# First weights and a head's inputs over a second DMA queue, with three more conversion ticks and one more head ahead of the first slot

## The chip, the cores and the metric

The kernel runs on one core of a Trainium2 chip. The core has TensorE (PE in the profile, with PEld for its weight loads), VectorE (DVE), ScalarE (ACT), GpSimd (POOL) and SyncE (SP), which here only issues DMAs. The metric is the device time of one execution in microseconds. Of the kernel before, three runs gave 1000.1 (median), 998.52 and 1000.47.

## The reference, cut to what matters

Three stages follow each other. Causal attention over 4 batches, 8 heads, 576 positions and head size 64, with an extra bias made of running sums:

```python
scores = scale * np.matmul(q, k.transpose(0, 1, 3, 2))
cum = np.cumsum(np.maximum(s, 0.0), axis=-1)
bias = -(cum[:, :, :, None] - cum[:, :, None, :])
scores = np.where(causal, -1e9, scores + np.minimum(bias, 0.0))
attn = softmax(scores)          # row maximum taken off, 1e-9 added to the sum
x = np.matmul(attn, v)          # heads side by side: 2304 tokens x 512
```

Then two feed-forward layers, 512 to 2048 to 512 each, over the 2304 tokens: the first with `g = h * clip(h + 3, 0, 6) / 6`, the second with `g = h * sigmoid(h)`. The weights come in as 64-bit floats.

## The kernel before, in words

**Weights.** A layer's two matrices are cut into 16 chunks of rows each, called i0 to i15 and o0 to o15. A chunk of the first layer is 128 x 512 64-bit words, 512 KB. It is loaded raw by one DMA (line 147), and then turned into a high and a low 32-bit part: ScalarE takes the two 32-bit halves apart (lines 159 and 160), GpSimd makes the sign (line 161), VectorE joins them (lines 172 and 176), ScalarE rounds the high part (line 120) and VectorE forms the low part (line 187). The class `Feed` does this as a pipeline: one call of `tick` (line 200) loads a new chunk, takes apart the chunk of three ticks ago, joins the one of four ticks ago and splits the one of five ticks ago. So the first three ticks only issue loads. The intermediate `mag` tiles come from a pool of three.

**Attention.** The 4 x 8 heads are each cut in two parts, A (positions 0 to 255) and B (the rest), and are worked through one per slot. A head's inputs are loaded by `load` (q, k and v, three DMAs for the first 14 heads, lines 413, 414 and 403) and `load_cum` (the running sums, line 423, from the on-chip tile `pairs` for heads 0 to 3, from its copy `pair_d` in memory after that). In `slot` (line 787) a head goes through its scores (line 512), the masked row minimum (line 534), the exponential (line 552), transposes (line 580) and the product with v (line 687). The tile `pairs` is written by VectorE (line 349) and ScalarE (line 350) from a scan of s (line 345).

**Order.** Nine slots hold attention only. Their number of ticks comes from a rate of 0.4 a slot; afterwards each slot has two ticks, and beside its head a step of the first layer: `first` (lines 260 to 262) multiplies by an i chunk, `gate_high` and `gate_low` make the activation, `second` (lines 299 to 301) multiplies by an o chunk. When the heads have run out, the rest of the first layer and then the whole second layer follow, all on TensorE. Before all that, line 91 issues 34 matmuls on a constant tile, and slots without a step issue three more each (line 825). `split_rows` (line 352) writes six rows of running sums to memory (line 365), for use by later heads.

**Queues.** Every DMA ahead of the very end is issued by SP, in one order, and all transfers use one queue. The head inputs of the first 14 heads lie in the places of chunks 8 to 15, and the tiles of the running sums in places of chunks 6, 7 and 15, so the raw loads of those chunks come after their use. The order of instructions on each engine is made by a list scheduler: an instruction that is ready in the scheduler's model can be placed ahead of one that stands earlier in the source (the cast of line 362, which stands behind slot 9, runs at 4.96 us).

Of the kernel before, what the change touches and what calls it, by code (L numbers as in the profile page):

```python
# [11 lines left out]
I32 = mybir.dt.int32  # L12
# [15 lines left out]
def kernel(  # L28
# [15 lines left out]
    nc = tc.nc  # L44
# [85 lines left out]
    class Chunk:  # L130
        def __init__(self, kind, m, f):
            self.key = (kind, m, f)
            self.src = ((w1i, w1o), (w2i, w2o))[m][kind == "o"][f]
            self.nm = f"{kind}{m}_{f}"
            self.home = wpool, f"{kind}{f}"
# [2 lines left out]
            pool, tag = self.home  # L138
            return pool.tile(shape, dt, tag=tag, name=f"{name}{self.nm}")

        def load(self):
            if self.src.dtype == F32:
                self.val = self.place([P, DM], F32, "raw")
                nc.sync.dma_start(self.val, self.src)
            else:
                raw = self.place([P, 2 * DM], I32, "raw")
                nc.sync.dma_start(raw, self.src.bitcast(I32))
                words = raw.rearrange("p (n two) -> p n two", two=2)
                self.words = words[:, :, 0], words[:, :, 1]

# [38 lines left out]
    class Feed:  # L189


        def __init__(self, keys, hi_eng, lo_eng):
            self.ch = [Chunk(*k) for k in keys]
            self.hi_eng, self.lo_eng = hi_eng, lo_eng
            self.t = 0

        def done(self):
            return self.t >= len(self.ch) + 3 + 2

        def tick(self):  # L200
            n = len(self.ch)
            t = self.t - 3
            lo = self.lo_eng[t % len(self.lo_eng)] if 0 <= t - 2 < n else ""
            if lo:
                self.ch[t - 2].high(self.hi_eng[t % len(self.hi_eng)])
            if 0 <= t < n:
                self.ch[t].fields()
            if lo == "p":
                self.ch[t - 2].low(lo)
            if 0 <= t - 1 < n:  # L210
                self.ch[t - 1].join()
            if lo == "v":
                self.ch[t - 2].low(lo)
            if self.t < n:
                self.ch[self.t].load()
            self.t += 1


# [133 lines left out]
    def split_rows():  # L352

        def row(tag, name):
            return wpool.tile([BH, S], F32R, tag=tag, name=name)

        f = NF - 1
        hi, lo = row(f"i{f}", "cumh"), row(f"o{f}", "cuml")
        one, neg = row(f"i{NF // 2 - 2}", "one"), row(f"i{NF // 2 - 1}", "neg")
        nc.gpsimd.memset(f32(one), 1.0)  # L360
        nc.gpsimd.memset(f32(neg), -1.0)
        nc.scalar.copy(hi, crow)
        nc.vector.tensor_tensor(out=lo, in0=crow, in1=f32(hi), op=ALU.subtract)
        for r, t in enumerate((one, one, hi, lo, neg, neg)):
            nc.sync.dma_start(f32(rows_d[:, r, :]), f32(t))
# [4 lines left out]
    class Head:  # L370
# [20 lines left out]
                    (c, 0, w // 2, False), (c, w // 2, w, True)]  # L391
            self.full = [c for c in self.chunks if c < NFULL]

        def load(self):
            b, h, nm, nk, nq = self.b, self.h, self.nm, self.nk, self.nq
            if self.at < 14:

                t = wpool.tile([P, 2 * DM], F32, tag=spare[self.at], name=f"in{nm}")
                self.q2, self.k2 = t[:, :nq], t[:, nq : nq + nk]
                self.qk = t[:, : nq + nk]  # L400
                self.va = t[:, DM + nk :][:, : self.nkc * D].rearrange("p (c d) -> p c d", d=D)
                self.load_qk()
                nc.sync.dma_start(self.va, v1[b, h, :, : self.nkc, :])
                return
            tags = ("qs", "kl") if self.whole and self.slot else ("q2", "k2")
            self.q2 = apool.tile([P, nq], F32, tag=tags[0], name=f"q2{nm}")
            self.k2 = apool.tile([P, nk], F32, tag=tags[1], name=f"k2{nm}")
            self.load_qk()

        def load_qk(self):  # L410
            b, h, nk = self.b, self.h, self.nk
            for r in (slice(0, D), slice(D, 2 * D))[: 1 if self.whole else 2]:
                nc.sync.dma_start(self.q2[r, :], qT[b, h, :, self.q0 : nk])
                nc.sync.dma_start(self.k2[r, :], kT[b, h, :, :nk])

        def load_cum(self):

# [356 lines left out]
    heads = []  # L774
# [3 lines left out]
    feed = Feed([(kd, 0, f) for f in range(NF) for kd in "io"], "a", "v")  # L778
# [3 lines left out]
    def ticks(n):  # L782
        for _ in range(n):
            if not feed.done():
                feed.tick()
# [79 lines left out]
    def at(i):  # L865
        return heads[i] if 0 <= i < len(heads) else None


    loaded = 2
    for hd in heads[:loaded]:  # L870
        hd.load()
    ticks(3)
    for hd in heads[:loaded]:
        hd.load_cum()
    nc.sync.dma_start(pair_d, pairs)
    heads[0].places()
    k = 0
    p1 = p2 = None
    plan = [(True, False)] * (H + 1) + [(i < 55, True) for i in range(68)]
    nslot = 0  # L880
    for has_head, has_step in plan:
        cur = at(k) if has_head else None
        nx = at(k + 1) if has_head else None
        loads = []
        while has_head and loaded < len(heads) and loaded <= k + (
            2
        ):
            loads.append(heads[loaded])
            loaded += 1
        k += has_head and cur is not None  # L890
        tk = [0, 0, 0, 0]
        if not feed.done():
            rate = ((0.4,)*9+(2,))[min(nslot, len(((0.4,)*9+(2,))) - 1)]
            for i in range(4):
                feed_at += rate / 4
                tk[i] = int(feed_at)
                feed_at -= tk[i]
        slot(cur, p1, p2, nx, loads, has_step, tk)
        if nslot == 9:
            split_rows()  # L900
        p1, p2 = cur, p1
        nslot += 1
        if nslot == H + 1:
            p2.av_sum()
            p2 = None
            split1(0)
            turns["s"] = turns["s"][:1]
        if has_step and step in first_step[1:NB1]:
            blk = first_step.index(step)
            assert k - (cur is not None) >= (blk + 1) * H  # L910
            if p2:
                p2.av_sum()
                p2 = None
            if blk == NB1 - 1:
                cx.close()
                xpool = cx.enter_context(
                    tc.tile_pool(name="xlast", bufs=1, side="right", reuse_waits="tile")
                )
            split1(blk)
            if blk == NB1 - 1:  # L920
                break
# [70 lines left out]
    feed = Feed([("o", 1, f) for f in range(NF)], "a", "v")  # L992
# [293 lines left out]
```

## Time and profile before

| | |
|---|---|
| median of three runs | 1000.1 us |
| profiled execution | 1000.54 us, its span 998.8 us |
| PE busy | 970.8 us (97%) |
| DVE busy | 737.9 us (74%) |
| ACT busy | 511.0 us (51%) |
| POOL busy | 317.2 us (32%) |
| DMA moved | 125.41 MB, mean 126 GB/s |

The span runs from the first to the last instruction; the profiled execution's own time has 1.7 us around it. The busy shares are means over stages of very different kind, so the table alone does not say which engine a stage waits for. A busy PE can be one that multiplies a constant tile.

### The profile page before, as it was taken

Reading aid. Unit: us, or ns where it says so; the run is one execution under the profiler, and the core shown is the slowest. Engines: PE = TensorE matmul, PEld = TensorE weight load, DVE = VectorE, ACT = ScalarE, POOL = GpSimd, SP = SyncE. Lnnn points to the kernel's source line nnn. Section 1 sums busy time; section 2 is a strip of 40 time slices with the busy share of each in tenths; the row PEclk is TensorE's granted clock in tenths of the full one; section 3 lists DMA queues with packets and bytes.
Section 4 is the critical chain, followed back from the end, with each engine's and each line's share of the span. In section 5 each row is a group of like instructions: output and inputs, shape, how many; then the busy total and the mean of one; then the engine's idle time right before and its main releaser. Section 6 shows DMA issues by size and latency. Waiting matters only on the chain.

```text
span 998.8 us, 17929 instructions
## 1 busy us (share of the span) xinstructions
PE 970.8 (97%) x6268; PEld 891.6 (89%) x6268; DVE 737.9 (74%) x1757; ACT 511.0 (51%) x1177; POOL 317.2 (32%) x323
## 2 busy tenths in 40 slices
PE   8899989999999999999999999999999999999997
PEld 5789979999999999999997877899988989889996
DVE  6899998888789888988866799887574434743343
ACT  6898554555455555555446656564443323432332
POOL 4457853443333443434425566532000000000000
PEclk9999999999999999999999999999999999999999
DMA  5796112312222223222215957434354233442421
GB/s 174 225 302 198 47 40 67 92 46 63 83 77 75 71 59 92 60 64 80 60 39 186 392 212 237 163 116 190 133 195 169 77 145 110 167 154 76 148 74 64
DMA packets 54419, 125.41 MB, mean 126 GB/s; under 512 B 12332, under 2 KB 34076, under 8 KB 51000
## 3 DMA queue, kind: packets, MB, share of 16 engines
q1 hardware_dynamic: 53880, 123.60, 37.3%
q8 instruction: 50, 0.82, 0.3%
q10 hardware_dynamic: 448, 0.66, 0.2%
q14 instruction: 41, 0.34, 0.1%
HBM read 99.52 MB, written 24.69 MB: 124 GB/s over the span
## 4 chain that ended last, share of the span: by engine, by line
PE 70%; DVE 11%; DMA 8%; issue 4%; POOL 4%; SPq 3%; ACT 1%; POOLq 0%; DVEq 0%; ACTq 0%
PE a L1083 6%; PE a L1084 6%; PE a L1085 6%; PE h L1066 5%; PE h L1068 5%; PE h L1067 5%; PE ph L260 4%; PE ph L261 4%; PE ph L262 4%; PE acc L299 4%; PE acc L300 4%; PE acc L301 4%; PE poB L672 4%; DMA rawi<-in_w1i_dram 3%; POOL rawo L161 2%
## 5 line engine op out<-in xcount | busy, mean ns | idle before, releaser
L260 PE MATMUL ph<-xh,wi 128*128 128x256 f32 (+1 forms) x512 | 154.1, 303 | 3.2 <-DVE g L273 3.1
L300 PE MATMUL acc<-gl,wo 128*128 128x256 f32 (+1 forms) x512 | 151.1, 297 | 2.4 <-DVE gl L280 2.4
L261 PE MATMUL ph<-xl,wi 128*128 128x256 f32 (+1 forms) x512 | 151.6, 296 | 0.0
L262 PE MATMUL ph<-xh,wi 128*128 128x256 f32 (+1 forms) x512 | 151.3, 296 | 0.0
L301 PE MATMUL acc<-gh,wo 128*128 128x256 f32 (+1 forms) x512 | 149.8, 294 | 0.0
L1125 ACT ACTIVATE gh<-h 128x384 fp32r<-128x384 f32 x96 | 50.3, 524 | 185.4 <-DVE h L1133 185.3
L299 PE MATMUL acc<-gh,wo 128*128 128x256 f32 (+1 forms) x512 | 143.8, 297 | 0.0
L1083 PE MATMUL a<-wo,gh 128*128 128x512 f32 x288 | 113.5, 394 | 1.4 <-ACT gh L1125 0.9
L1084 PE MATMUL a<-wo,gh 128*128 128x512 f32 x288 | 113.1, 393 | 0.0
L260 PEld LDWEIGHTS ph<-xh,wi 128*128 128x128 f32 x512 | 97.4, 190 | 8.9 <-DVE g L273 2.5
L300 PEld LDWEIGHTS acc<-gl,wo 128*128 128x128 f32 x512 | 96.4, 188 | 6.4 <-DVE gl L280 3.5
L262 PEld LDWEIGHTS ph<-xh,wi 128*128 128x128 f32 x512 | 97.6, 191 | 3.0
L261 PEld LDWEIGHTS ph<-xl,wi 128*128 128x128 f32 x512 | 97.5, 190 | 3.2
L301 PEld LDWEIGHTS acc<-gh,wo 128*128 128x128 f32 x512 | 96.5, 189 | 3.3
L299 PEld LDWEIGHTS acc<-gh,wo 128*128 128x128 f32 x512 | 95.6, 189 | 3.4
L161 POOL TENSOR_SCALAR rawi<-rawi 128x512 int32<-128x512 f32 x32 | 70.0, 2188 | 74.1 <-ACT magi L160 48.4
L1085 PE MATMUL a<-wo,gl 128*128 128x512 f32 x288 | 90.0, 392 | 0.0
L161 POOL TENSOR_SCALAR rawo<-rawo 128x512 int32<-128x512 f32 x32 | 74.5, 2329 | 48.0 <-ACT mago L160 46.3
L1127 DVE TENSOR_TENSOR gl<-h,gh 128x384 fp32r<-128x384 f32 x96 | 53.8, 560 | 39.9 <-ACT h L1126 38.2
L114 POOL TENSOR_SCALAR gh<-g 128x512 fp32r<-128x512 f32 x68 | 50.6, 745 | 92.6 <-DVE g L273 77.4
L1133 DVE TENSOR_TENSOR h<-h,u 128x384 f32<-128x384 f32 x72 | 40.1, 557 | 53.5 <-PE h L1068 53.2
L1066 PE MATMUL h<-x0t,w 128*128 128x384 f32 x192 | 64.9, 338 | 0.7 <-DVE u L1133 0.7
(220 smaller groups left out, 2554.6 us busy)
## 6 DMA issues: line engine op xcount, KB each, us to landing
w<-w_d SPq DMA_DIRECT2D x18, 1792.0 KB
w_d<-w SPq DMA_DIRECT2D x8, 1792.0 KB
k2B<-in_kT_dram SPq DMA_DIRECT2D x64, 144.0 KB
rawi<-in_w1i_dram SPq DMA_DIRECT2D x16, 512.0 KB
rawo<-in_w1o_dram SPq DMA_DIRECT2D x16, 512.0 KB
rawi<-in_w2i_dram SPq DMA_DIRECT2D x16, 512.0 KB
rawo<-in_w2o_dram SPq DMA_DIRECT2D x16, 512.0 KB
q2B<-in_qT_dram SPq DMA_DIRECT2D x64, 80.0 KB
```

The lines of the kernel that those rows point to most:

```text
L161: nc.gpsimd.tensor_scalar(out=high, in0=f32(high), scalar1=0.0, scalar2=float(SIGN), op0=ALU.is_lt, op1=ALU.mult,)
L260: nc.tensor.matmul(o, wih[:, cs], xh[c], start=c == 0, stop=False)
L261: nc.tensor.matmul(o, wih[:, cs], xl[c], start=False, stop=False)
L262: nc.tensor.matmul(o, wil[:, cs], xh[c], start=False, stop=c == NDC - 1)
L299: nc.tensor.matmul(a, woh[:, cs], gh[:, jj, :], start=b0, stop=False)
L300: nc.tensor.matmul(a, woh[:, cs], gl[:, jj, :], start=False, stop=False)
L301: nc.tensor.matmul(a, wol[:, cs], gh[:, jj, :], start=False, stop=b1)
L1066: nc.tensor.matmul(ps, w[:, 0, cs], xh[:, c, :], start=c == 0, stop=False)
L1083: nc.tensor.matmul(accs[t], gh[:, k, cs], woh, start=b0, stop=False)
L1084: nc.tensor.matmul(accs[t], gh[:, k, cs], wol, start=False, stop=False)
L1085: nc.tensor.matmul(accs[t], gl[:, k, cs], woh, start=False, stop=b1)
L1127: nc.vector.tensor_tensor(out=gl[:, i, o], in0=g, in1=f32(gh[:, i, o]), op=ALU.subtract)
```

## The change

The loads get a queue as an argument. Before the first slot, head 0 and head 2 load over SP's queue and head 1 over ScalarE's. All raw chunks that are loaded before the tenth slot go over ScalarE's queue; afterwards over SP's again. Three ticks precede the loads of the running sums as before, and three more follow them, ahead of slot 0, so that six ticks are done instead of three and six raw chunks are loaded instead of three. Until 14 heads are loaded, a slot loads the head three ahead instead of two. `split_rows` comes behind the eighth slot instead of the tenth.

```diff
-        def load(self):
+        def load(self, queue=nc.sync):
             if self.src.dtype == F32:
                 self.val = self.place([P, DM], F32, "raw")
-                nc.sync.dma_start(self.val, self.src)
+                queue.dma_start(self.val, self.src)
             else:
                 raw = self.place([P, 2 * DM], I32, "raw")
-                nc.sync.dma_start(raw, self.src.bitcast(I32))
+                queue.dma_start(raw, self.src.bitcast(I32))
...
+            self.queue = nc.sync
...
-                self.ch[self.t].load()
+                self.ch[self.t].load(self.queue)
...
-                self.load_qk()
-                nc.sync.dma_start(self.va, v1[b, h, :, : self.nkc, :])
+                self.load_qk(queue)
+                queue.dma_start(self.va, v1[b, h, :, : self.nkc, :])
...
-                nc.sync.dma_start(self.q2[r, :], qT[b, h, :, self.q0 : nk])
-                nc.sync.dma_start(self.k2[r, :], kT[b, h, :, :nk])
+                queue.dma_start(self.q2[r, :], qT[b, h, :, self.q0 : nk])
+                queue.dma_start(self.k2[r, :], kT[b, h, :, :nk])
...
-    loaded = 2
-    for hd in heads[:loaded]:
-        hd.load()
+    loaded = 3
+    feed.queue = nc.scalar
+    for hd, queue in zip(heads, (nc.sync, nc.scalar, nc.sync)):
+        hd.load(queue)
     ticks(3)
     for hd in heads[:loaded]:
         hd.load_cum()
     nc.sync.dma_start(pair_d, pairs)
+    ticks(3)
     heads[0].places()
...
-        while has_head and loaded < len(heads) and loaded <= k + (
-            2
-        ):
+        while has_head and loaded < len(heads) and loaded <= k + 2 + (loaded < 14):
...
-        if nslot == 9:
+        if nslot == 7:
             split_rows()
...
         if nslot == H + 1:
+            feed.queue = nc.sync
             p2.av_sum()
```

## Rows read from the trace of the kernel before

**Rows 1.** The page: share of the chain that ended last, by engine

```profile
PE 70%; DVE 11%; DMA 8%; issue 4%; POOL 4%; SPq 3%; ACT 1%; POOLq 0%; DVEq 0%; ACTq 0%
```

**Rows 2.** Windows of seven stretches: start and end, length, busy time by engine

```profile
core 0: us, PE busy (x) PEld busy (x) DVE busy (x) ACT busy (x) POOL busy (x), PEclk, DMA share, GB/s
0.00:5.00 5.00, 3.56 (x9) 1.34 (x10) 2.78 (x5) 1.63 (x3) 3.67 (x17) 1.00 0.25 68
5.00:12.03 7.03, 6.68 (x31) 3.06 (x29) 1.14 (x3) 3.48 (x7) 1.95 (x2) 1.00 0.86 290
12.03:31.10 19.07, 15.93 (x110) 12.51 (x108) 16.77 (x71) 15.71 (x50) 8.49 (x5) 1.00 0.51 140
31.10:40.00 8.90, 7.76 (x58) 6.63 (x57) 7.78 (x29) 7.85 (x23) 3.47 (x2) 1.00 0.84 249
40.00:80.00 40.00, 36.87 (x280) 34.65 (x279) 38.57 (x119) 37.42 (x94) 24.93 (x13) 0.96 0.91 284
80.00:150.50 70.50, 63.24 (x496) 59.29 (x494) 69.12 (x156) 45.46 (x105) 47.04 (x34) 0.98 0.29 87
150.50:998.80 848.30, 836.75 (x5295) 774.13 (x5295) 601.75 (x1381) 399.44 (x900) 227.62 (x254) 1.00 0.35 119
```

**Rows 3.** Chain of waits around 150 us: start, length, what

```profile
149.88 0.61 DVE g L273
150.48 0.04 issue
150.53 0.38 PE ph L260
```

**Rows 4.** Timeline of PE, two places: start, length, engine, line, work, idle before

```profile
1.45 9.63 PE L86 MATMUL idle<-busy 128*128 128x512 bf16 x34 [1.45 <-DVE half L101]
11.42 0.46 PE L512 MATMUL ps0A<-inA 66*128 66x128 f32 x2 [0.35 <-DMA rawi<-in_w1i_dram]
...
27.34 0.46 PE L512 MATMUL ps0A<-inA 66*128 66x128 f32 x2 [1.45 <-DMA inA<-pair_d]
```

**Rows 5.** Timeline of SP, the DMA issues, from the start

```profile
0.73 0.41 SPq L341 DMA_DIRECT2D irow<-in_s_dram  x1
1.20 0.58 SPq L413 DMA_DIRECT2D inA<-in_qT_dram  x1
1.83 0.58 SPq L414 DMA_DIRECT2D inA<-in_kT_dram  x1
2.45 0.58 SPq L403 DMA_DIRECT2D inA<-in_v_dram  x1
...
4.86 0.43 SPq L147 DMA_DIRECT2D rawi<-in_w1i_dram  x1
...
6.42 1.39 SPq L423 DMA_DIRECT2D inA<-pairs  x2
...
35.41 0.78 SPq L365 DMA_DIRECT2D rows_d<-one  x2
...
37.25 0.84 SPq L365 DMA_DIRECT2D rows_d<-neg  x2
```

**Rows 6.** Timeline of ACT and POOL before the first slot

```profile
0.72 1.28 ACT L350 ACT_TABLE_LOAD   x1 [0.72 <-PEq L1267]
4.65 0.40 ACT L350 COPY pairs<-orow 32x256 f32<-32x256 f32 x1 [2.65 <-DVE orow L345]
9.02 0.67 ACT L159 ACTIVATE rawi<-rawi 128x512 int32<-128x512 uint32 x1 [3.39 <-DMA rawi<-in_w1i_dram]
10.33 2.00 POOL L161 TENSOR_SCALAR rawi<-rawi 128x512 int32<-128x512 f32 x1 [5.08 <-DMA rawo<-in_w1o_dram]
```

**Rows 7.** Timeline of DVE, opening and head 7

```profile
2.64 0.60 DVE L342 TENSOR_SCALAR irow<-irow 32x576 f32<-32x576 f32 x1 [1.25 <-DMA irow<-in_s_dram]
12.03 0.29 DVE L534 CUSTOM_DVE_ANT_0 pb0A<-ps0A,cmask 128x128 f32<-128x128 f32 x1 [5.62 <-PE ps0A L512]
12.37 1.13 DVE L172 SCALAR_TENSOR_TENSOR magi<-magi,rawi 128x512 int32<-128x512 int32 x1
...
25.36 0.69 DVE L187 TENSOR_TENSOR wo<-mago,wo 128x512 fp32r<-128x512 f32 x1
25.96 0.28 DVE L694 TENSOR_TENSOR xtA<-poA,sums 128x128 f32<-128x128 f32 x1
27.84 0.29 DVE L534 CUSTOM_DVE_ANT_0 pb0A<-ps0A,cmask 128x128 f32<-128x128 f32 x1 [1.59 <-PE ps0A L512]
```

**Rows 8.** Chain of waits, two places where SP's queue stands

```profile
5.81 5.79 DMA rawi<-in_w1i_dram
11.60 0.02 issue
11.61 0.48 SPq L413
...
28.91 4.46 DMA rawo<-in_w1o_dram
33.38 0.02 issue
33.39 0.47 SPq L414
```

More of the change, by code (lines that the diff above doesn't have):

```diff
@@ L392, in __init__, with load @@
             self.full = [c for c in self.chunks if c < NFULL]
-        def load(self):
+        def load(self, queue=nc.sync):
             b, h, nm, nk, nq = self.b, self.h, self.nm, self.nk, self.nq
@@ L408, in load, with load_qk @@
             self.load_qk()
-        def load_qk(self):
+        def load_qk(self, queue=nc.sync):
             b, h, nk = self.b, self.h, self.nk
             for r in (slice(0, D), slice(D, 2 * D))[: 1 if self.whole else 2]:
-                nc.sync.dma_start(self.q2[r, :], qT[b, h, :, self.q0 : nk])
-                nc.sync.dma_start(self.k2[r, :], kT[b, h, :, :nk])
+                queue.dma_start(self.q2[r, :], qT[b, h, :, self.q0 : nk])
+                queue.dma_start(self.k2[r, :], kT[b, h, :, :nk])
         def load_cum(self):
```

## The prediction

> **What bounds the kernel now.** I read the chain by engine first: PE holds 70% of it, DVE 11%, DMA 8%, SP's queue 3% [rows 1]. So most of the time is TensorE's own, and the change doesn't touch it. The windows say where the rest lies [rows 2]. From 150.5 us to the end PE is busy 836.75 of 848.3 us: whatever ends before 150.5 moves this block as a whole, and nothing in it gets shorter. From 40 to 150.5 DVE is busy 38.57 + 69.12 = 107.69 of 110.5 us, while PE idles 10.4. The chain of waits changes from DVE to PE at 150.5, and all of the last DVE pieces lie end to end there [rows 3]. So up to 150.5 the bound is VectorE: a fixed amount of work (conversion of 32 chunks, the soft-max, splits, gates) plus the time in which VectorE has none. The change removes none of the work. It can gain only what VectorE idles.
>
> That idle time is: up to 12.03, when the first soft-max starts, 12.03 - 2.78 - 1.14 = 8.1 us; from 12.03 to 31.1, 19.07 - 16.77 = 2.3; from 31.1 to 40, 1.1; from 40 to 80, 1.4; from 80 to 150.5, 1.4 [rows 2]. The question is how much of it three more raw chunks and a shorter SP queue can fill.
>
> **The opening.** Before, SP issues the loads one after the other: s at 0.73, head 0 in three DMAs of 0.58 us (1.85 with the gaps), head 1 likewise, and raw chunk 0 only at 4.86 [rows 5]. ScalarE takes chunk 0 apart at 9.02, GpSimd does its sign from 10.33 for 2.00 us, and VectorE joins it at 12.37 [rows 6, 7]. From 6.4 to 12.03 VectorE waits 5.62 us with nothing to do [rows 7].
>
> After, ScalarE issues head 1 (1.85 us, by SP's rows for the same DMAs) and then raw 0. If these come ahead of ScalarE's table load, raw 0 is issued at 0.72 + 1.85 = 2.57; behind it, at 2.00 + 1.85 = 3.85. Against 4.86 that is 2.3 or 1.0 us earlier, and the DMA engines are busy only 0.25 of the first 5 us [rows 2], so I let the landing and the chain of ACT, POOL and DVE move as much: the first join comes at 10.1 to 11.4, and I take the middle, 10.75. So VectorE starts on 1.6 us of work that it had to do later. The bound on the better side is 2.3. On the other it is 0, if VectorE's order keeps the join behind the first soft-max as now.
>
> The first slot itself hardly moves. The 34 matmuls on the constant tile keep PE until 1.45 + 9.63 = 11.08, and the first scores start at 11.42, with 0.35 us of waiting for a DMA [rows 4]. So however early head 0 arrives, at most 0.35 us is gained there, and I count it as nothing, since VectorE is then working on joins.
>
> Could it get later? The running sums of head 0 are loaded from 6.42 on, behind three raw chunks in one queue [rows 5], and PE's wait ends with the landing of a raw chunk [rows 4]. Raw 0 has landed when ScalarE starts at 9.02 and raw 2, issued at 5.81, lands at 11.60 [rows 6, 8], so a raw chunk takes about (11.60 - 9.02) / 2 = 1.3 us. Six of them from an early landing of 7.4 end at 7.4 + 5 x 1.3 = 13.9. Sums that waited behind all six would let the first slot start 2.5 us later than 11.42. At the other end stands the unloaded row: s is issued at 0.73 and used at 2.64, 1.9 us later [rows 5, 7], so sums issued at 6.42 would be there at 8.3. I take the second, since raw chunks no longer stand ahead of the sums in SP's order, and keep 2.5 us for the range.
>
> The Trainium skill, on the page "DMA: Bandwidth & Descriptors", section "Queues, rings and completion order", says that SP and ScalarE each own a row of rings, and that each DMA engine goes round-robin between the rows that have work, a packet at a time. By that rule the sums pass the raw chunks and this step costs 0; by the one-queue behaviour that this trace shows it costs 2.5 us. No run here shows two queues loaded at once.
>
> **ScalarE's issuing.** Three head DMAs and up to nine raw ones leave SP for ScalarE: 1.85 + 9 x 0.47 = 6.1 us of its time. ScalarE idles 12.03 - 1.63 - 3.48 = 6.9 us up to 12.03, which hides it; from 12.03 to 31.1 it idles 3.4 us more [rows 2]. The three raw loads that the source places inside the slots cost 1.4 us if they delay an exponential there. I take 0, bounded by 1.4. The copy of line 350, without which the running sums can't be loaded, has to wait if DMA issues precede it on ScalarE. It ran at 4.65 [rows 6]; there are 11.08 - 1.9 = 9.2 us until PE could notice, so 2 to 3 us of delay cost nothing.
>
> **The slots up to 31 us.** The largest gap of VectorE here is 1.59 us, at 27.84, behind PE's 1.45 us at 27.34, which waits for head 7's sums [rows 4, 7]. These are late because SP works off four DMAs a head plus the raw ones, after it stood until 11.60 for raw 2 [rows 8]. After, SP has no raw DMA until the tenth slot, and head 2 is loaded up front; the 0.47 us of each of two raw issues and the hold at 11.60 are gone, several microseconds in all. I take the whole gap, 1.6 us; what comes next is VectorE itself. Bounds: 0, if another wait on the same engine takes its place, and 2.3, all idle time of the stretch.
>
> **From 31 to 80 us.** The DMA engines are busy 0.84 and 0.91 of the time here, with raw chunks [rows 2]. Three chunks of 1.3 us are out of the way earlier, so some of VectorE's 1.1 + 1.4 us should close. I take 0.4, bounded by 0 and 2.5.
>
> **The rest.** `split_rows` two slots earlier puts six DMAs (35.41 to 38.09, [rows 5]) ahead of the loads of two heads. Heads are loaded at least a slot ahead, which covers it; with the cover gone it would be 2.7 us of SP, so up to 1 us on the chain. The third head ahead costs nothing: the first 14 heads have places of their own. PE's clock is granted at 0.96 to 1.00 in all these stretches, near its 2.4 GHz level, and I see no reason for a change.
>
> Sum: -1.6 (opening) + 0 (first slot) + 0 (ScalarE) - 1.6 (head 7) - 0.4 (31 to 80) = -3.6 us. All of it comes ahead of 150.5, and passes to the end one for one, since the long block after that is PE's. The profiled execution took 1000.54 (998.8 of span and 1.7 around it), 0.4 above the median of the runs, 1000.1; against that median the forecast is **996.5 us**.
>
> **Rivals.**
>
> *A, slower: ScalarE is held by its own loads.* SP's issue at 11.61 comes right when raw 2, eight issues earlier, has landed, and the one at 33.39 right when the raw chunk issued at 28.91, eight issues earlier, has landed [rows 8]: a DMA is not issued before the eighth before it is done. If the list scheduler puts all raw loads ahead of the copy of line 350 on ScalarE, the later ones wait there for landings of the earlier. The copy then runs when raw 1 or 2 has landed, 8.7 to 10.0; sums are issued about 1.3 us later, land 1.9 after that, and the first slot starts at 11.9 to 13.2, up to 1.8 late. The next heads' loads queue behind raw 5 to 8, four landings of 1.3, another 5 us against now. Conversions fill part of the gap, one per 2.00 us of GpSimd. I price it at +2.4, so **1002.5**. It decides if the first scores come later than about 13 us. Against it: only the first six raw loads precede slot 0 in the source.
>
> *B, no change: the order hardly moves.* The scheduler is already ahead of the source: four chunks are fully converted by 26 us, the last at 25.36 [rows 7], where three plus 0.4 a slot ask for one. More ticks in the source may then move nothing on VectorE, the change would not do what it says, and only half of head 7's gap would go: -0.8, so **999.3**. For it also speaks a rule of the Trainium skill, same page, section "Issuing engines are not separate DMA queues": all issuers run on the same 16 DMA engines, and issuing from several saves only issue time. The trace agrees so far as the engines are busy 0.86 from 5 to 12 us [rows 2].
>
> *C, more: every gap before 80 us that raw chunks or SP can close is closed.* 2.3 + 2.3 + 2.5 = 7.1, so **993.0**.
>
> **How the numbers follow.** The forecast (994.5 to 998.1) has 0.47, C 0.13, B 0.23, A 0.17. A measurement of this kernel tells about 0.2% from no change, 2 us, so faster means below 998.1 and slower above 1002.1. Faster: the forecast, C, a little of B, less an edge: 0.61. Same: most of B, and the milder half of A: 0.25. Slower: 0.14. The range goes from 993.0, where C lies, to 1001.8, which takes in B and half of A.
>
> **What would show it.** Right: the first join of line 172 near 10.75 and ahead of the first line 534; the first scores of line 512 at 11.1 to 11.4; no wait of PE of 1 us for a head's sums up to slot 8; VectorE's idle time up to 40 us at 8 instead of 11.5; the change from DVE to PE in the chain at 147. Wrong: the copy of line 350 later than 8 us, or first scores later than 13 (A); joins and switch where they were (B). The whole reasoning fails if the block after the switch gets longer or shorter by itself.

## The result and the profile after

The changed kernel takes 1004.7 us (median of 15 runs, 1001.74 to 1010.67). The kernel before takes 1000.18 beside it (15 runs, 997.44 to 1004.77). The ratio is 1.0051, with a 95% interval from 1.0033 to 1.0069. The forecast was 996.5, so the sign was wrong: 4.5 us more in place of 3.6 less. The profiled execution took 1005.12 with a span of 1003.3, which is 4.5 more than the 998.8 of before, and the pages below can account for it. Lines of the changed kernel stand one or two higher: 261 to 263 are the first layer's step, 513 the scores, 535 the soft-max, 553 the exponential, 581 the transposes, 424 the loads of running sums.

The page's chain by engine answers to [rows 1]: SP's queue is gone from it, VectorE has 14% instead of 11%.

```profile
PE 72%; DVE 14%; DMA 6%; issue 4%; POOL 4%; ACT 1%; SPq 0%; POOLq 0%; DVEq 0%; ACTq 0%
```

The windows answer to [rows 2], with the same columns; so do all windows below.

```profile
core 0: us, PE busy (x) PEld busy (x) DVE busy (x) ACT busy (x) POOL busy (x), PEclk, DMA share, GB/s
0.00:5.00 5.00, 3.56 (x11) 1.41 (x12) 2.81 (x5) 1.64 (x2) 3.67 (x17) 1.00 0.39 107
5.00:12.03 7.03, 6.20 (x31) 3.09 (x30) 0.48 (x2) 2.93 (x6) 2.34 (x3) 1.00 0.94 342
12.03:31.10 19.07, 15.26 (x61) 12.04 (x60) 17.55 (x55) 16.64 (x45) 12.15 (x6) 0.56 0.61 204
31.10:40.00 8.90, 6.21 (x39) 4.98 (x38) 8.90 (x26) 5.69 (x17) 4.36 (x2) 0.88 0.51 120
40.00:80.00 40.00, 36.91 (x249) 33.82 (x247) 34.63 (x109) 37.39 (x94) 19.37 (x10) 0.85 0.93 323
80.00:150.50 70.50, 68.69 (x575) 66.93 (x574) 68.45 (x178) 45.57 (x111) 42.80 (x34) 1.00 0.19 52
150.50:998.80 848.30, 840.42 (x5314) 777.97 (x5312) 604.69 (x1387) 401.84 (x907) 227.02 (x255) 1.00 0.35 118
```

VectorE's idle time up to 150.5 is what the forecast lived on. Before it was 14.3 us. Here it is 8.7 in the first two windows, 1.5, 0.0, 5.4 and 2.1, together 17.7. In sum 3.3 us came on top: up to 40 us it fell from 11.5 to 10.3, where the forecast asked for 8, and behind that it grew from 2.8 to 7.4. What did get better is TensorE from 80 to 150.5: it idles 1.8 us instead of 7.3, and the chain goes over from VectorE to TensorE at 128.5, not at 147 as forecast or at 150.5 as before [rows 3]:

```profile
127.40 1.06 DVE gl L281
128.46 0.04 issue
128.50 0.38 PE acc L301
```

So the conversions were done earlier, as the change asks, and the time was lost ahead of that. The places to look at are the opening of TensorE, to be read against [rows 4], and its clock. PE's timeline (start, length, engine, line, work, idle before):

```profile
11.09 0.46 PE L513 MATMUL ps0A<-inA 66*128 66x128 f32 x2 [0.83 <-DMA inA<-pairs]
...
12.04 0.60 PE L513 MATMUL ps1A<-inA 66*128 66x256 f32 x2
16.34 0.45 PE L581 MATMUL pt0A<-ident,pb0A 128*128 128x128 f32 x1 [3.71 <-ACT pb0A L553]
...
42.27 0.56 PE L261 MATMUL ph<-xh,wi 128*128 128x256 f32 x1
```

The scores start at 11.09, where they were forecast. Then TensorE stands for 3.71 us until the first exponential has run, and its first feed-forward step starts at 42.27. Before, these two were at 12.76 (ScalarE) and 31.14 (TensorE):

```profile
12.76 0.39 ACT L552 ACTIVATE pb0A<-pb0A,mxA 128x128 f32<-128x128 f32 x1
```

```profile
31.14 0.36 PE L260 MATMUL ph<-xh,wi 128*128 128x256 f32 x1
```

ScalarE's timeline shows what the exponential stands behind (against [rows 6]):

```profile
0.72 0.56 ACTq L414 DMA_DIRECT2D inA<-in_qT_dram  x1
...
4.65 0.40 ACT L351 COPY pairs<-orow 32x256 f32<-32x256 f32 x1 [0.65 <-DVE orow L346]
4.65 0.34 ACTq L147 DMA_DIRECT2D rawi<-in_w1i_dram  x1
...
8.62 0.67 ACT L159 ACTIVATE rawi<-rawi 128x512 int32<-128x512 uint32 x1 [3.57 <-DMA rawi<-in_w1i_dram]
...
11.57 0.68 ACT L159 ACTIVATE rawi<-rawi 128x512 int32<-128x512 uint32 x1 [0.48 <-DMA rawi<-in_w1i_dram]
...
14.61 0.62 ACT L120 CAST wi<-magi 128x512 fp32r<-128x512 f32 x1 [0.78 <-DVE mxA L535]
15.14 0.67 ACT L363 CAST cumh<-orow 32x576 fp32r<-32x576 f32 x1
15.71 0.40 ACT L553 ACTIVATE pb0A<-pb0A,mxA 128x128 f32<-128x128 f32 x1
```

Its own three head DMAs come first, then the table load, the copy of line 351 (at 4.65, as before) and the raw issues. The copy waits for VectorE's scan of s, and the first raw load behind it is issued at 4.65, where the forecast had 2.57 to 3.85. The first chunk is taken apart at 8.62, 0.4 earlier. From 8.62 to 15.71 ScalarE takes four chunks apart or in part, issues five raw loads, rounds chunk 0 and casts the running sums (at 4.96 before) before it gets to the exponential. VectorE does its part of the same (against [rows 7]):

```profile
11.94 1.12 DVE L172 SCALAR_TENSOR_TENSOR magi<-magi,rawi 128x512 int32<-128x512 int32 x1 [6.55 <-POOL rawi L161]
...
13.70 0.28 DVE L535 CUSTOM_DVE_ANT_0 pb0A<-ps0A,cmask 128x128 f32<-128x128 f32 x1
```

The first join runs at 11.94, ahead of the first soft-max, which starts at 13.70 instead of 12.03. VectorE's split of the running sums (line 364), which lay in its idle opening at 5.66 before, needs ScalarE's late cast and comes at 17.03. And SP (against [rows 5, 8]) still stands: the load of v of a later head, behind the row at 11.57, is issued at 15.88.

```profile
5.53 1.97 SPq L424 DMA_DIRECT2D inA<-pairs  x3
...
11.57 0.60 SPq L415 DMA_DIRECT2D inA<-in_kT_dram  x1
15.88 0.36 SPq L404 DMA_DIRECT2D inA<-in_v_dram  x1
```

In the chain that ended last, the way to the first step runs over VectorE, with some pieces of ScalarE between 22.93 and 26.12, from a raw chunk's landing to 38.43: joins, splits and soft-max end to end. The exponential at 15.71 is not in it.

```profile
9.89 5.97 DMA rawo<-in_w1o_dram
15.87 0.01 issue
15.87 0.68 DVE mago L172
...
38.22 0.21 DVE xtA L695
38.43 0.04 issue
38.48 0.69 PE pxA L706 x2
```

The granted clock of the changed kernel in windows of 1 us, from that stretch of 3.71 us on:

```profile
13.00:14.00 1.00, 0.00 (x0) 0.00 (x0) 0.96 (x5) 0.69 (x1) 1.00 (x2) 1.00 1.02 418
14.00:15.00 1.00, 0.00 (x0) 0.00 (x0) 0.34 (x2) 0.39 (x1) 1.00 (x1) 0.68 1.08 374
15.00:16.00 1.00, 0.00 (x0) 0.00 (x0) 0.74 (x2) 1.00 (x3) 0.82 (x1) 0.50 0.97 316
...
30.00:31.00 1.00, 1.00 (x6) 0.93 (x5) 1.00 (x3) 0.45 (x1) 0.25 (x1) 0.50 0.32 90
...
32.00:33.00 1.00, 1.00 (x10) 0.78 (x8) 1.00 (x4) 0.58 (x2) 1.00 (x1) 1.00 0.27 79
...
40.00:41.00 1.00, 1.00 (x6) 0.57 (x3) 0.79 (x7) 1.00 (x3) 0.00 (x0) 0.50 0.54 205
```

TensorE does nothing from 12.6 to 16.3; the granted clock goes from 1.00 to 0.50, which is the step from 2.4 to 1.2 GHz, and stays there to 31 us although TensorE is busy almost all the time from 16.3 on. After another stop of 2 us, from 34.5 to 36.5, it is at 0.50 once more from 39 to 45. The six products of one head (line 688) last 1.54 us at that level, at 40.43, and 0.78 at the other, at 48.34.

### The profile page after: what moved, and what is told of

The parts are those of the page before. It is cut to its first block, busy times and chain, and to the rows that moved or that the text cites. A ratio compares the mean times of both kernels' runs of the same rounds, so it can differ in the third digit from the quotient of the medians.

```text
span 1003.3 us, 17950 instructions
## 1 busy us (share of the span) xinstructions
PE 977.2 (97%) x6268; PEld 900.2 (90%) x6268; DVE 737.7 (74%) x1757; ACT 511.7 (51%) x1177; POOL 311.7 (31%) x323
## 4 chain that ended last, share of the span: by engine, by line
PE 72%; DVE 14%; DMA 6%; issue 4%; POOL 4%; ACT 1%; SPq 0%; POOLq 0%; DVEq 0%; ACTq 0%
PE a L1085 6%; PE a L1086 6%; PE a L1087 6%; PE h L1068 5%; PE h L1070 5%; PE h L1069 5%; PE ph L261 4%; PE ph L262 4%; PE ph L263 4%; PE acc L301 4%; PE acc L300 4%; PE acc L302 4%; PE poB L673 3%; POOL rawo L161 2%; DMA rawi<-in_w2i_dram 2%
## 5 line engine op out<-in xcount | busy, mean ns | idle before, releaser
L161 POOL TENSOR_SCALAR rawi<-rawi 128x512 int32<-128x512 f32 x32 | 67.7, 2115 | 79.8 <-ACT magi L160 46.9
L114 POOL TENSOR_SCALAR gh<-g 128x512 fp32r<-128x512 f32 x68 | 49.8, 734 | 94.8 <-DVE g L274 79.7
```

Of the source, the lines that this page charges most:

```text
L161: nc.gpsimd.tensor_scalar(out=high, in0=f32(high), scalar1=0.0, scalar2=float(SIGN), op0=ALU.is_lt, op1=ALU.mult,)
```

## Experiments

Sixteen kernels ran, all timed in five rounds beside the kernel before on the same chip. Each edit also lets the list scheduler lay the instructions anew, on all engines; only e6 and e7 keep the order of their parent. The texts on record use these names. D: conversions placed ahead of the first step push it back on VectorE, and TensorE can't make it up. K: the lost clock is the cost. Q: the raw loads on ScalarE's queue are. T: the time is the start of the first feed-forward step, TensorE's idle time and lost clock after it, and a fixed rest. V: the prediction's premise, VectorE's idle time before 150 us is what counts. O: the opening is the cause, that is conversions ahead of the first exponential, TensorE's stop and the clock.

**The change taken apart.** e2: the kernel before with the second three ticks.

```diff
     nc.sync.dma_start(pair_d, pairs)
+    ticks(3)
     heads[0].places()
```

> The kernel before with three more ticks ahead of slot 0 and nothing else: all loads on SP's queue, two heads ahead, rows of sums as before. Theory D: about as many chunks are converted ahead of the first step as in the changed kernel, the first step starts near 40 us, the time is 1003 to 1006. Rival K: the first soft-max stands ahead of the first join again, TensorE doesn't idle, the clock stays at 1.00 from 12 to 31 us, and the time is 999 to 1001. Rival Q: no load on ScalarE, so 999 to 1001.

Measured 1006.0, ratio 1.0044 [1.0023, 1.0064]. VectorE splits the activations for the first step in four pieces (line 726); eleven chunks are fully converted ahead of the fourth piece, where before had six. The first step is at 42.3. Time and first step are as D had them, but K is not decided against, since the clock fell here too: TensorE stops for 3.11 us on a head's running sums, and the clock is 0.82 and 0.69 in the two windows from 12.03 to 40. The first exponential is not late (12.76 before):

```profile
12.57 0.39 ACT L552 ACTIVATE pb0A<-pb0A,mxA 128x128 f32<-128x128 f32 x1
```

```profile
23.05 0.76 PE L512 MATMUL ps0A<-inA 66*128 66x128 f32 x2 [3.11 <-DMA inA<-pair_d]
```

f4: the kernel before with raw loads and head 1 on ScalarE's queue.

```diff
     loaded = 2
-    for hd in heads[:loaded]:
-        hd.load()
+    feed.queue = nc.scalar
+    for hd, queue in zip(heads[:loaded], (nc.sync, nc.scalar)):
+        hd.load(queue)
```

> The kernel before with raw loads up to the tenth slot and head 1 on ScalarE's queue, three ticks and two heads as before: the queue edit alone. The list order then puts ten full conversions ahead of the splits, as in the changed kernel, without the second three ticks. Theory T: the first step at 40 to 43 us, TensorE's idle time behind it 5 to 8 and lost clock 4 to 8, so 1002 to 1007. Theory V: VectorE's idle time in the opening closes as the prediction had it, 996 to 998.

Measured 1009.62, 1.0081 [1.0062, 1.0101], above even T's range; first step 38.8. V's 996 to 998 is missed by more: the opening's idle time of VectorE did not close, with 8.9 us up to 12.03 against 8.1. Ten conversions now stand ahead of the fourth piece of activations, without one more tick; that the scheduler puts them there because the raw chunks land earlier in its model is the likely reason. As in e2 the first soft-max stands ahead of the first join, and the first exponential is early, so a late exponential is not needed for a late first step:

```profile
12.61 0.40 ACT L553 ACTIVATE pb0A<-pb0A,mxA 128x128 f32<-128x128 f32 x1 [0.22 <-DVE mxA L535]
```

f3: three heads up front, on SP, and three ahead.

```diff
-    loaded = 2
+    loaded = 3
...
-        while has_head and loaded < len(heads) and loaded <= k + (
-            2
-        ):
+        while has_head and loaded < len(heads) and loaded <= k + 2 + (loaded < 14):
```

> The kernel before with three heads loaded up front on the one queue, and three ahead until 14 are loaded; nothing else. Theory T: 12 more conversions are not there (six ahead of the splits, as before), but three more DMAs stand ahead of the raw loads; the first step at 31 to 34, 999 to 1003. Theory V: the conversions start 1.9 us later in VectorE's idle time, +1 to +2, 1001 to 1002.

Measured 1001.86, 1.0018 [1.0002, 1.0033], inside the ranges of both theories.

f2: `split_rows` behind the eighth slot.

```diff
-        if nslot == 9:
+        if nslot == 7:
```

> The kernel before with split_rows behind the eighth slot instead of the tenth, nothing else. Both theories: the first step stays at 31 to 32 and six chunks stand ahead of the splits, so 999 to 1001; if the six DMAs delay two heads' loads, TensorE's idle time before 40 us grows by up to 2.7 and the time with it, 1002 to 1003.

Measured 1008.54, 1.0073 [1.0055, 1.0091]; neither had that. The first step is at 30.1, not late. TensorE's waits from 31 to 80 us show one for a head's running sums (us in total, times, longest), as `split_rows` changes what stands ahead of their loads on SP; before, no such wait reaches 0.7 us there. It lasts from 77.4 to 79.7, and the granted clock is at 0.50 behind it.

```profile
PE ps0A L512 <- DMA q2A<-pair_d: 2.3, 1, 2.3
```

```profile
78.00:80.00 2.00, 0.33 (x3) 0.36 (x4) 2.00 (x6) 2.00 (x7) 1.56 (x1) 1.00 0.82 273
...
82.00:84.00 2.00, 2.00 (x9) 1.82 (x9) 1.27 (x5) 0.67 (x1) 1.76 (x1) 0.50 0.11 32
```

So no part gains by itself, and the parts don't add up: 0.44, 0.81, 0.18 and 0.73% against 0.51% for all.

**One part of the change undone.** e1: without the second three ticks.

```diff
     nc.sync.dma_start(pair_d, pairs)
-    ticks(3)
```

> The changed kernel without its second three ticks ahead of slot 0; both queues, the third head and the earlier running-sum rows stay. The changed kernel's first feed-forward matmul started at 42.3 us against 31.1 before, with nine chunks fully converted ahead of it against four. Theory D (dose: conversions ahead of the first step push it back on VectorE, and TensorE, which has only some 11 us of idle time left behind it, can't make that up): fewer conversions stand ahead, the first step starts at 31 to 36 us, the time is 997 to 1001. Rival K (clock: the first exponential stands behind conversions on ScalarE, TensorE idles over 3 us at 12 to 16 us and is granted half its clock up to 31 us): the first join still stands ahead of the first soft-max, so the clock still falls, 1003 to 1005. Rival Q (queue: the raw loads on ScalarE hold it and SP): unchanged, 1003 to 1005.

Measured 1006.54, 1.0050 [1.0029, 1.0072]. A miss for D: seven chunks stand ahead of the splits instead of ten, and the first step is still at 41.7, at a granted clock of 0.61 and 0.50 in the two windows ahead of it. K and Q, with 1003 to 1005, come nearest.

e4: all loads on SP.

```diff
-    feed.queue = nc.scalar
-    for hd, queue in zip(heads, (nc.sync, nc.scalar, nc.sync)):
+    for hd, queue in zip(heads, (nc.sync, nc.sync, nc.sync)):
```

> The changed kernel with every load on SP's queue; six ticks ahead of slot 0, the third head and the earlier rows of sums stay. The first soft-max stands ahead of the first join again, and nine chunks are converted ahead of the first step's last split. Theory K: no long idle time of TensorE at 12 to 16 us, so less clock lost than in the changed kernel; a mean clock of 0.99 or more and 999 to 1002. Rival D: the first step at 40 us, 1003 to 1006. Rival Q (loads on ScalarE are what costs): 999 to 1001.

Measured 1007.18, 1.0070 [1.0045, 1.0095]. With nothing on ScalarE's queue it is no faster; with e2, Q falls. The first step is at 42.1, and the time is above D's range. K is not tested, for the clock fell here as well, to 0.73 and 0.50 in the two windows from 12.03 to 40.

e8: without the second ticks and with the raw loads on SP; head 1 on ScalarE, the third head and the early `split_rows` stay.

```diff
-    feed.queue = nc.scalar
...
-    ticks(3)
     heads[0].places()
```

> The changed kernel with neither the raw loads on ScalarE nor the second three ticks: head 1 alone over ScalarE's queue, three heads ahead, the rows of sums two slots earlier. The order at the start is the soft-max first, with six chunks converted ahead of the first step's last split, as before. All theories: 999 to 1001. By the term of the forecast for head 7 (1.6 us) it would be 998.5 to 1000.

Measured 1006.67, 1.0055 [1.0036, 1.0075]: a miss for all. The first step is at 31.8, but the granted clock is 0.82 from 12 to 31 us and again from 40 to 80.

e5: no ticks in the first nine slots.

```diff
-            rate = ((0.4,)*9+(2,))[min(nslot, len(((0.4,)*9+(2,))) - 1)]
+            rate = ((0.0,)*9+(2,))[min(nslot, len(((0.0,)*9+(2,))) - 1)]
```

> The changed kernel with its six ticks ahead of slot 0, but none in the first nine slots (a rate of 0 instead of 0.4 there), so that fewer chunks stand ahead of the first step by the source's order. Theory D: the first step starts at 31 to 36 us, the time is 997 to 1001, like that without the second three ticks. Rival K: the opening is the same as in the changed kernel, TensorE idles at 12 to 16 us, 1003 to 1005. Rival Q: three raw loads less on ScalarE, six stay, 1002 to 1005.

Measured 1004.78, 1.0038 [1.0018, 1.0058]; first step 38.5, clock 0.58 from 12 to 31 us. A miss for D as well; inside the ranges of K and Q.

g1: `split_rows` back behind the tenth slot.

```diff
-        if nslot == 7:
+        if nslot == 9:
```

> The changed kernel with split_rows back behind the tenth slot. If split_rows is the cause: 998 to 1001. Theory O (the opening is the cause): it stays at 1003 to 1007, first step 41 to 43 us.

Measured 1007.89, 1.0064 [1.0042, 1.0085]; the first step is at 41.9, as O had it, and the time 0.9 above O's range. `split_rows`, dear by itself, is not the cause here.

**The clock.** e6: the kernel before, the order on every engine unchanged, with fewer matmuls on the constant tile.

```diff
-keep_clock(34, ...)
+keep_clock(26, ...)
...
-keep_clock(3, heads_of(p1.prob[1]))
+keep_clock(1, heads_of(p1.prob[1]))
```

> The kernel before with 26 instead of 34 matmuls on the constant tile ahead of the first scores, and one instead of three in each slot without a step; every engine's order of work is otherwise that of the kernel before. TensorE then idles some 2.5 us ahead of the first scores and more within the slots. Over the runs so far, time and mean granted clock go together, about 6 us for 0.01 of clock, in each kernel. Theory K (the lost clock costs the time, whatever the order): if the granted clock falls in 12 to 40 us, the time rises by 3 to 6 us, to 1004 to 1007. Rival D (the conversions' place ahead of the first step costs it, the clock only goes along): at most 1 us, 1000 to 1002, even with a lower clock, since TensorE has idle time there. If the clock does not fall, nothing is told.

Measured 1002.41, 1.0019 [0.9998, 1.0040], between K's and D's, and an interval that just reaches 1. PE's timeline and the windows:

```profile
11.54 0.46 PE L512 MATMUL ps0A<-inA 66*128 66x128 f32 x2 [1.77 <-DMA inA<-pairs]
```

```profile
12.03:31.10 19.07, 18.90 (x77) 16.06 (x77) 15.16 (x63) 14.02 (x44) 8.33 (x4) 0.54 0.54 164
```

After the stop of 1.77 us the clock is 0.54 in the window from 12.03, though TensorE is busy 18.90 of its 19.07 us. The first step comes at 34.5 instead of 31.1. So with every order kept the lower clock costs 3.4 us at the first step, with two matmuls on the constant tile less in each of these slots, and some 2 us (0 to 4) at the end.

e3: the changed kernel with ten more such matmuls behind the scores of head 1.

```diff
         exps(0)
+        if cur is heads[1]:
+            with tc.issue_after(cur.last.ins):
+                keep_clock(10, heads_of(feed.ch[0].mag))
```

> The changed kernel with ten more matmuls on a constant tile behind the first two heads' scores, to fill TensorE's idle time from 13.8 to 16.3 us; the order of the other work stays nearly as it is (ten chunks fully converted ahead of the first step's last split, as in the changed kernel). Rival K: the clock stays at or near 1.00 from 12 to 31 us and the time falls to 999 to 1001. Theory D: with the clock held, the slots get a little faster, by the halved durations of transposes and small products, 1 to 2 us; the first step still starts at 39 us or later, and the time is 1002 to 1004.5. Rival Q: 1003 to 1005.

Measured 1008.2, 1.0071 [1.0051, 1.0090]. The clock is better from 12 to 31 us (0.73 instead of 0.56) and worse from 40 to 80 (0.66 instead of 0.85). The time is above all three ranges. The clock was not held, so this tells nothing against K.

e7: 40 opening matmuls instead of 34, the order unchanged.

```diff
-keep_clock(34, ...)
+keep_clock(40, ...)
```

> The changed kernel with 40 instead of 34 matmuls on the constant tile at the start; every engine's order of work is otherwise that of the changed kernel. The first scores start some 1.5 us later, and TensorE's idle time behind them shrinks from 3.7 to about 2.2 us. Theory K: if the clock stays up from 14 to 31 us, the time is 998 to 1001. Rival D: 1003 to 1006, with the clock up too. If the clock falls as before, both expect 1003 to 1006, and nothing is told.

Measured 1003.16, 1.0043 [1.0021, 1.0065]; the clock fell all the same (0.59 from 12 to 31 us). Inconclusive.

**The opening.** f1 goes the other way from the change: one tick less ahead of the first slot.

```diff
-    ticks(3)
+    ticks(2)
```

> The kernel before with two ticks instead of three ahead of the first slot, nothing else: four chunks instead of six stand ahead of the first splits on VectorE. Theory T (the time is the start of the first feed-forward step, TensorE's idle time and lost clock after it, and a fixed 938 us of TensorE's work): the first step at 27 to 29 us instead of 31.1; TensorE's idle time behind it rises from 11.5 by up to 4 because chunks are late; sum 997 to 1001. Theory V (the prediction's premise, VectorE's idle time before 150 us is what counts): one chunk less in the opening leaves VectorE 2 us more without work there, so slower by about 2, 1002 to 1003.

Measured 1013.7, 1.0108 [1.0085, 1.0130]. Slower is V's sign, five times V's price; T missed. The windows:

```profile
12.03:31.10 19.07, 17.16 (x125) 14.14 (x124) 17.02 (x75) 15.92 (x52) 5.83 (x3) 1.00 0.56 163
...
40.00:80.00 40.00, 36.52 (x261) 33.80 (x260) 37.14 (x117) 34.59 (x88) 21.34 (x10) 0.91 0.80 256
80.00:150.50 70.50, 61.95 (x452) 58.97 (x452) 61.84 (x142) 44.95 (x101) 46.25 (x35) 0.90 0.31 98
```

The first step is at 29.5 and the clock whole up to 31.1. Behind that TensorE idles 14.5 us up to 160 instead of 11.5, and the clock is 0.90 to 0.91 all the way from 40 to 150.5. Fewer early conversions would show in both; the run does not separate them from the rest of the new order.

g2: the changed kernel, as many ticks, but the conversions of the first nine slots stand behind the slot's exponential on ScalarE.

```diff
     nc.sync.dma_start(pair_d, pairs)
-    ticks(3)
+    ticks(1)
...
         exps(0)
+        if cur is heads[0]:
+            with tc.issue_after(cur.last.ins):
+                ticks(2)
...
-        ticks(tk[0])
+        if not mm and cur and nslot < 9:
+            with tc.issue_after(cur.last.ins):
+                ticks(tk[0])
+        else:
+            ticks(tk[0])
```

Here `last` is the slot's exponential; `ticks(tk[1])` to `ticks(tk[3])` are wrapped alike.

> The changed kernel with as many ticks, but conversions of the first nine slots stand behind the slot's exponential on ScalarE. Theory O: first exponential near 13 instead of 15.7, TensorE's 3.7 us of idle time gone, clock at its upper level up to 31 us, first step 37 to 39, and 999 to 1002. If the opening is not the cause: 1003 to 1007.

Measured 1004.86, 1.0033 [1.0014, 1.0051], not told apart from the changed kernel, and O's 999 to 1002 is missed. The exponential runs at 13.55, but the second one waits behind conversions in its place, and PE's timeline shows a stop of 2.00 us there; the clock is 0.60 from 12 to 31 us.

```profile
17.34 0.69 PE L581 MATMUL pt0A<-ident,pb1A 128*128 128x128 f32 x2 [2.00 <-ACT pb1A L553]
```

g3: as g2, without the two ticks in slot 0, so that four precede it.

```diff
-        if cur is heads[0]:
-            with tc.issue_after(cur.last.ins):
-                ticks(2)
```

> As g2, with four ticks instead of six ahead of the first slot and none added in it, so six full conversions ahead of the splits as in the kernel before. Theory O: first step 31 to 34 with the clock held, 997 to 1000, since the first join also stands ahead of the first soft-max. If fewer early conversions starve TensorE later: 1003 to 1008, with its idle time from the first step to 160 us above 11.5.

Measured 1001.18 beside 1001.34 of before, 1.0002 [0.9985, 1.0020], wholly below the interval of the changed kernel. First exponential and windows of g3:

```profile
14.51 0.40 ACT L553 ACTIVATE pb0A<-pb0A,mxA 128x128 f32<-128x128 f32 x1 [3.28 <-DVE mxA L535]
```

```profile
12.03:31.10 19.07, 15.80 (x101) 12.85 (x102) 13.24 (x63) 14.17 (x46) 4.69 (x3) 0.91 0.50 153
31.10:40.00 8.90, 7.51 (x53) 6.06 (x52) 8.30 (x30) 8.90 (x25) 7.27 (x4) 1.00 0.62 192
40.00:80.00 40.00, 34.57 (x241) 32.75 (x240) 39.52 (x105) 37.70 (x87) 26.48 (x13) 0.83 0.98 339
80.00:150.50 70.50, 66.91 (x549) 64.09 (x548) 66.92 (x169) 45.52 (x113) 46.36 (x35) 1.00 0.17 47
```

The first step is at 31.4, the clock 0.91 up to there. The four exponentials of the first two heads follow each other, and TensorE has no stop over 0.9 us up to its first step. The queue, the third head, the early `split_rows` and a fourth tick are all in it, so these don't make the loss in this order. g3 differs from g2 by two ticks, and from the changed kernel by these and by the place of the conversions; fewer ticks alone (e1) and the place alone (g2) did not bring the first step back. O's time of 997 to 1000 was missed by one: the loss goes, a gain does not appear.

g4: as g3, with `split_rows` behind the tenth slot.

```diff
-        if nslot == 7:
+        if nslot == 9:
```

> As g3, with split_rows back behind the tenth slot. Theory O: as g3. If split_rows is the cause: 4 to 7 us below g3.

Measured 1004.64, 1.0036 [1.0016, 1.0056], 3.5 above g3; both theories missed. Its opening is no worse than g3's: the first exponential is at 13.61, the clock 1.00 up to 40 us and the first step at 30.0; from 40 to 80 the clock is 0.79. So a good opening alone does not make the kernel fast. The same edit costs 0.7% in f2 one way and 0.3% here the other way. No version that ran beats the kernel before.

**Two accounts.** By TensorE: the table sums windows of 2 to 10 us of each profiled execution: the start of the first step; TensorE's idle time and the lost clock (length times one minus the granted clock) from there to 160 us, and the two together from 160 to the end; and the rest of the span.

| | span | first step | idle | lost clock | both after 160 | rest |
|---|---|---|---|---|---|---|
| before | 998.8 | 31.1 | 11.5 | 3.4 | 13.1 | 939.6 |
| after | 1003.3 | 42.3 | 4.9 | 4.8 | 15.3 | 936.0 |
| e6 | 1000.2 | 34.5 | 11.1 | 3.4 | 10.2 | 941.1 |
| g3 | 1000.4 | 31.4 | 10.4 | 6.8 | 12.8 | 938.9 |
| f1 | 1013.4 | 29.5 | 14.5 | 12.0 | 16.2 | 941.2 |
| f2 | 1006.7 | 30.1 | 16.6 | 6.8 | 12.8 | 940.4 |

The rest is 936 to 941 in all 18 profiles. From before to after: 11.2 later at the first step, 6.6 won back from idle time, 1.4 + 2.2 lost behind it, and 3.6 less in the rest, together 4.6. The rest's spread of 5 us is the error of this account, and it is as large as the difference that is to be explained.

By VectorE: its idle time up to 150.5, which the prediction went by, goes with the spans of the 18 profiles (one execution each; correlation 0.71, about 0.9 us of span for each us of it), better than the start of the first step (-0.08) or the mean granted clock (-0.40). It is smallest in the kernel before, 14.3, and 17.7 in the changed kernel; in f4 and f1 it is 8.3 and 9.5 more than before, and their times are 0.81 and 1.08% longer. Single pairs go the other way: g3 has 18.6 and is 2.9 us shorter than the changed kernel. Which of the two is the cause, a VectorE without work or the TensorE that it waits for, no run separates.

## Why the prediction was wrong

**"It can gain only what VectorE idles", and the change would fill 3.6 us of it.** The filling is the step that failed. The sum needed VectorE's idle time up to 150.5 to fall from 14.3 to 10.7 us; it rose to 17.7, and the time rose by 4.5. Up to 40 us it fell by 1.3, from 40 to 150.5 it rose by 4.6. The forecast moved pieces into the gaps of an order that it took as fixed, but the change lays a new order. Nine full conversions stand ahead of the first step instead of four, of three VectorE pieces of 0.6 to 0.7 us each, about 10 us for the five more, and the first step came 11.2 us later, at the end of a chain of such pieces. Over the 18 profiles the first step is at 38.5 to 42.3 where six to nine conversions stand ahead of it, and at 29.5 to 34.5 where two to four do, but for g2 with four and 36.8. A late step also leaves time for more of them, so the count is an argument and no proof. By e6 some 3.4 of the 11.2 are the clock. TensorE had 11.5 us of idle time behind its first step to win back, and won 6.6.

The premise that the time follows VectorE's idle time is not what failed: 3.3 us more of it and 4.5 us more time fit each other, as the second account has it. But how much of the 4.5 is the late step, the clock, or later waits stays open: e8, f1, f2 and g4 lose 0.4 to 1.1% with the first step at 29.5 to 31.8.

**Opening, -1.6.** Failed. Raw 0 was issued at 4.65 and not at 2.57 to 3.85, behind ScalarE's copy, so the join came 0.4 earlier and not 1.6, at 11.94. VectorE's idle time up to 12.03 rose from 8.1 to 8.7, since the split of the running sums left it. The join came ahead of the first soft-max, as forecast, and I booked it as work moved into idle time. It made the soft-max 1.7 us late, and with the conversions on ScalarE the exponential 2.95; TensorE stood for 3.71, and its clock fell. I had asked what fills VectorE's gap, not who waits for what then stands behind it. It is not the only way to the loss: e2 and f4 have the soft-max first and lose 0.44 and 0.81%.

**First slot, 0.** Right for the scores (11.09, forecast 11.1 to 11.4), but partly by luck: the 34 matmuls ended at 10.26, not at 11.08, and TensorE then waited 0.83 for head 0's running sums. The slot's next link was late all the same.

**ScalarE's issuing, 0, at most 1.4.** The issues cost little by themselves (0.33 to 0.72 us each). But f4 shows what comes of the loads that they start: ten conversions ahead of the activations' fourth piece and 0.8% by this edit alone. The size was off because I priced the DMA issues and not the conversions that become ready.

**Sums behind raw chunks, 0.** No later in the end, but not by the landing that was forecast: issued at 5.53, while four raw chunks were issued on the other queue (4.65 to 6.00), the sums were used at 11.09 after the wait of 0.83, 5.5 us after their issue where the text had 1.9. The raw chunk issued at 5.52 was taken up at 11.57 after a wait for it, so the sums passed it by about 0.5 us.

**Head 7, -1.6, and 31 to 80 us, -0.4.** Head 7's wait is gone, the longest waits for running sums from 11 to 42 us being 0.8. From 12.03 to 31.1 VectorE's idle time fell by 0.8, half of the term, while TensorE ran at 0.56 of its clock. From 31.1 to 40 it fell by 1.1, and from 40 to 80 it rose by 3.9, in waits for TensorE: 2.8 more for a term of -0.4.

**The rest, 0.** `split_rows` has no fixed price: f2 shows 0.7% by itself, with a wait of 2.3 us for a head's sums where the text gave up to 1 us, and a clock that falls behind it; g4 shows the other sign, and g1 is too close to the changed kernel to tell. "PE's clock ... I see no reason for a change" failed outright: the mean granted clock fell from 0.995 to 0.982. In the 15 runs of the changed kernel the time falls by 6.9 us for each 0.01 that the mean clock rises (correlation -0.95), in 100 runs of the kernel before by 5.7 (-0.77). Across the orders it does not carry over: f2, with 0.993, is 0.73% slower.

**The block after 150.5 passes one for one.** Nearly: to 998.8 TensorE idles 7.9 us of it, before 11.6.

**The rivals.** A had the sign and close to the size (1002.5), by a mechanism that did not happen: the copy stands at 4.65, the scores at 11.09. ScalarE was held, but mostly by conversions; of its own loads one issue of 0.33 us stands between the first soft-max and the exponential. B falls since the order changed much, C with the gaps that were not filled.

Open: why a good part of the orders lose clock later, from 40 to 150 us (e8, f1, f3, g4), and why g3, whose first step is back at 31.4, does not get the 3.6 us. Its lost clock of 6.8 us from the first step to 160, against 3.4, would be enough, but no run held it.

## What to carry to other kernels

When work is moved into an engine's idle time, list what then stands behind it on that engine and on the others that share the work, and price the first consumer on the bounding engine; a gap that is filled is not a gain before that is known. If a scheduler lays out the order, an earlier transfer can make work ready and so change the order: count the pieces that now come ahead of the critical chain, in e2 and f4 eleven and ten instead of six. Take a forecast of idle time that will be filled as one that can go either way: here 3.6 us less were forecast and 3.3 more came. And where the end is set by TensorE, write the time as its start plus its idle time plus its lost clock plus a rest, and look how far the rest holds (5 us here) before reading smaller differences from it.

## What the hardware showed

Within or shortly behind a stop of TensorE of 3.71 us in the changed kernel, 2.26 in f2, 2.00 in g2 and 1.77 in e6 the granted clock went to 0.50; around the one of 1.45 before head 7 in the kernel before it stayed at 1.00 [rows 2, 4]. Nor does it take one long stop: in e8 TensorE had none of 0.9 us ahead of its first step, and the clock still went to 0.50 near 20.5 us, behind two windows of 1 us, from 18 to 20, in which TensorE was busy 0.41 and 0.33. The 1.2 GHz level then outlasts the stop by far: in e6 TensorE was busy 99% of the window from 12 to 31 us, and the clock was 0.54 over it. In f2 one wait on a DMA was followed by both: its own 2.26 us, and products at half the clock up to some 87 us.
